# Taking the reciprocal of the softmax sums a little later, and scaling the weights behind the score copies

## The chip, the cores and the metric

The kernel runs on one core of one Trainium2 chip. The metric is the device time of one execution in microseconds (us). Five engines of the core work side by side, each through a queue of its own in a fixed order: TensorE (PE in the profile; PEld is its weight load), VectorE (DVE), ScalarE (ACT), GpSimd (POOL) and SyncE (SP, which here only issues DMAs). An instruction that waits holds up everything behind it in its queue.

## The reference

The reference has two stages, both in float32. The first is attention with a top-32 mask, for 8 batches of 8 heads, 576 positions and a head size of 64:

```python
scores = scale * np.matmul(q, k.transpose(0, 1, 3, 2))
kth = np.partition(scores, -top_k, axis=-1)[..., -top_k:-top_k + 1]
scores = np.where(scores >= kth, scores, -1000000000.0)
scores = scores - np.max(scores, axis=-1, keepdims=True)
attn = np.exp(scores)
attn = attn / (np.sum(attn, axis=-1, keepdims=True) + 1e-09)
return np.matmul(attn, v)
```

Its output, with the heads side by side, is x of 4608 x 512, and the second stage is a gated feed-forward block with a hidden width of 1536:

```python
g = x @ w_gate
silu = g * (1.0 / (1.0 + np.exp(-g)))
val = x @ w_val
return silu * val @ w_out
```

## The kernel before, in words

**Units.** The attention is cut into 160 units: 8 batches, 5 blocks of queries in each, 4 pairs of heads. The first four blocks of a batch have 128 queries, and such a unit treats two heads one after the other (two instructions of 128 x 576 wherever one head needs one). The fifth block has the last 64 queries; there the two heads of the pair share the 128 partitions, so that a unit has one "head". There are 128 units of two heads and 32 of one, and the 16 units in a row from one batch's start are followed by four single ones.

**Steps of a unit.** `scores` (L278) multiplies queries and keys on TensorE into four banks of PSUM (tile `s`, two for a single unit), and ScalarE copies them out to `sc` (L313, L299). `select` (L316) finds the 32 largest scores of each row on VectorE: four rounds of MAX8 (L328), which yields eight at a time, with MATCH_REPLACE8 (L332) between, which strikes those eight out and writes the rest to `e`. `penalize` (L338) has ScalarE scale the 32nd score (tile `top`, L344), form a penalty for everything below it (L348, into `e`), and GpSimd subtract the penalty from the scores (L351). `weigh` (L354) takes the exponential on ScalarE, in place in `e`, with the sum of each row as a side result in `tot` (L360), and adds the epsilon (L365). `normalize` (L368) takes the reciprocal of `tot` on VectorE (L372) and multiplies `e` by it on ScalarE (L375, one instruction for each head). `turn` (L377) transposes `e` on TensorE (tile `etps`, L387), copied out by ScalarE to `et` (L388). `values` (L398) multiplies by v, for two units together, into the bank `av` (L421), and ScalarE copies that to `xT` (L437), the input of the feed-forward block.

**Turns.** The main loop (L748) issues one turn after another. Turn n holds steps of several units: `select(n)`, `penalize(n - 1)`, `weigh(n - 1)`, and `turn(n - 2)`. In even turns it also holds `scores` of the units n + 1 and n + 2 and `values` of the units n - 4 and n - 3; odd turns have neither. The normalization of unit n - 1 is split over two turns: its reciprocal is the last VectorE instruction of turn n (`next(norm, None)`, L808), and its multiplications are run in turn n + 1 right behind `penalize` (`run(scaled)`, L772). Seen from turn n, ScalarE's queue so runs: top and penalties of unit n - 1, multiplications of unit n - 2, and then, in even turns, the four score copies of unit n + 1 and the copy of `av` to `xT`; then the exponentials of unit n - 1, the score copies of unit n + 2 in even turns, and the copies of the transposes of unit n - 2.

**Order and buffers.** All engines' queues keep the order in which the program issues (L817 to L830 chain the instructions of each engine but SP). `dve(k)` issues the next k steps of `select` for each head. `pieces` puts shares of the feed-forward block between (generator `feed`, L463; its matmuls are L477 for gate and value, L523 and L563 for the output), as many as a credit allows, which follows an estimate of each turn's other work. The attention's PSUM pool `ps_t` has five banks that are handed out in turn: two sets of four score banks in an even turn cannot both be there at once, so the second scores of that turn need banks that the copies of the first have freed. `e` has three buffers, `m` (the maxima) two.

**The first turns.** While the first units run, the feed-forward weights are loaded and rounded in pieces: a DMA into one of three buffers `w` (L106), three ScalarE instructions (L114, L116, L117), one on VectorE (L121), two on GpSimd (L122, L123). `early[0]()` (L779) issues the ScalarE part of such a piece inside the turn, ahead of the exponentials.

Of the kernel before, what the change touches and what calls it, by code (L numbers as in the profile page):

```python
# [25 lines left out]
def kernel(  # L26
# [174 lines left out]
    def rounding(n):  # L201
        for _ in range(n):
            next(weight, None)
# [70 lines left out]
    def n_heads(qt):  # L274

        return 1 if qt == J else 2

    def scores(n):  # L278
        b, qt, hp = units[n]
        slab = preps[b * NHP + hp]  # L280
        sc = work.tile([P, 2 * S], FP32, tag="sc", name="sc", bufs=3)
        halves = [slice(0, D), slice(D, P)]
        half = S // 2

        def bank():
            return ps_t.tile([P, 512], FP32, tag="t", name="s")


        if qt == J:
            banks = [bank() for _ in range(2)]  # L290
            for i, ps in enumerate(banks):
                for d in halves:
                    k0 = R + i * half
                    nc.tensor.matmul(  # L294
                        ps[d, 0:half], slab[d, S + R : S + 2 * R], slab[d, k0 : k0 + half]
                    )
            yield
            for i, ps in enumerate(banks):
                nc.scalar.copy(sc[:, i * half : (i + 1) * half], ps[:, 0:half])  # L299
        else:  # L300
            q0 = S + 2 * R + qt * P
            banks = []
            for i in range(2):
                for hh, d in enumerate(halves):
                    ps = bank()
                    banks.append((i + 2 * hh, ps))
                    k0 = (1 - hh) * R + i * half
                    nc.tensor.matmul(  # L308
                        ps[:, 0:half], slab[d, q0 : q0 + P], slab[d, k0 : k0 + half]
                    )  # L310
            yield
            for i, ps in banks:
                nc.scalar.copy(sc[:, i * half : (i + 1) * half], ps[:, 0:half])  # L313
        state[n] = dict(sc=sc)

    def select(n):  # L316

        nh = n_heads(units[n][1])
        sc = state[n]["sc"]
        m = small.tile([P, 2, TOP_K], FP32, tag="m", name="m", bufs=2)  # L320
        heads = [slice(t * S, (t + 1) * S) for t in range(nh)]
        e = work.tile([P, 2 * S], FP32, tag="e", name="e", bufs=3)
        state[n] |= dict(m=m, e=e, heads=heads)
        cur = sc
        rounds = TOP_K // 8
        for r in range(rounds):
            for t, hs in enumerate(heads):
                nc.vector.max(m[:, t, 8 * r : 8 * r + 8], cur[:, hs])  # L328
                yield
            if r < rounds - 1:  # L330
                for t, hs in enumerate(heads):
                    nc.vector.match_replace(  # L332
                        e[:, hs], m[:, t, 8 * r : 8 * r + 8], cur[:, hs], LOWEST
                    )
                    yield
                cur = e

    def penalize(n):  # L338

        st = state[n]  # L340
        sc, m, e, heads = st.pop("sc"), st.pop("m"), st["e"], st["heads"]
        nh = len(heads)
        top = small.tile([P, 2], FP32, tag="top", name="top")
        nc.scalar.mul(top[:, 0:nh], m[:, 0:nh, TOP_K - 1], BIG)  # L344
        bias = small.tile([P, 2], FP32, tag="bias", name="bias")
        nc.gpsimd.tensor_scalar_mul(bias[:, 0:nh], m[:, 0:nh, 0], -scale)
        for t, hs in enumerate(heads):
            nc.scalar.activation(  # L348
                e[:, hs], sc[:, hs], AF.Relu, bias=top[:, t : t + 1], scale=-BIG
            )  # L350
            nc.gpsimd.tensor_tensor(e[:, hs], sc[:, hs], e[:, hs], ALU.subtract)  # L351
        st["bias"] = bias

    def weigh(n):  # L354

        st = state[n]
        e, heads, bias = st["e"], st["heads"], st.pop("bias")
        tot = small.tile([P, 2], FP32, tag="tot", name="tot")
        for t, hs in enumerate(heads):
            nc.scalar.activation(  # L360
                e[:, hs], e[:, hs], AF.Exp, bias=bias[:, t : t + 1], scale=scale,
                accum_out=tot[:, t : t + 1],
            )
        nh = len(heads)
        nc.scalar.activation(tot[:, 0:nh], tot[:, 0:nh], AF.Identity, bias=eps[:])  # L365
        st["tot"] = tot

    def normalize(n):  # L368
        st = state[n]
        tot, e, heads = st.pop("tot"), st["e"], st.pop("heads")  # L370
        nh = len(heads)
        nc.vector.reciprocal(tot[:, 0:nh], tot[:, 0:nh])  # L372
        yield
        for t, hs in enumerate(heads):
            nc.scalar.mul(e[:, hs], e[:, hs], tot[:, t : t + 1])  # L375
# [83 lines left out]
    def flush(queue):  # L459
        while queue:  # L460
            queue.pop(0)()
# [201 lines left out]
    NU = len(units)  # L663
# [22 lines left out]
    def fetch(n):  # L686

        b, qt, hp = units[n]
        i = b * NHP + hp
        if qt == 0:  # L690
            yield from prep(i)
        if qt == J and i + NHP < len(pairs):
            load(i + NHP)

    def share(n):


        others = 0.0
        costs = [(m, 0.7) for m in scored(n) + valued(n)] + [(n - TURN, 0.6)]
        for m, cost in costs:  # L700
            if m >= 0:
                others += cost * (0.5 if units[m][1] == J else 1)
        if units[n + 3][1] == 0:
            others += 0.6

        beside = 6.4 if T[1] else 7.0
        return beside * n_heads(units[n][1]) / 2 - others

    def scored(n):

        ahead = [n + 1] if n < 2 else [] if n % 2 else [n + 1, n + 2]
        return [m for m in ahead if m < NU]

    def valued(n):

        behind = [] if n % 2 else [n - 4, n - 3]
        return [m for m in behind if 0 <= m < NU]

    def pieces(n):
        for _ in range(n):  # L720
            if credit[0] >= 1:
                credit[0] -= piece()

    def run(steps):
        for _ in steps:
            pass

    def finish_units(ns):
        values(ns)
        for n in ns:  # L730
            b, qt, hp = units[n]
            if qt == J and b + 1 < B:
                load_v((b + 1) * NHP + hp)
# [8 lines left out]
    load(2)  # L742
    credit = [0.0]
    no = iter(())
    scaled = no
    TURN = 2
    due = [2.0]
    for n in range(NU + 3):  # L748
        nh = n_heads(units[n][1]) if n < NU else 1
        topk = select(n) if n < NU else no  # L750
        norm = normalize(n - 1) if 0 <= n - 1 < NU else no
        nxt = [scores(m) for m in scored(n)]
        ahead = fetch(n + 3 if n else 2) if n + 3 < NU else no

        def dve(k, beside=True):

            for _ in range(k * nh):
                next(topk, None)
                due[0] += 5 / 6 if beside else 0
                if due[0] >= 1:  # L760
                    due[0] -= 1
                    rounding(1)

        if n >= NU - NHP:
            credit[0] = 8.0
        else:
            credit[0] = min(credit[0] + share(n), share(n) + 1)
        flush(on_act)
        if 0 <= n - 1 < NU:
            penalize(n - 1)  # L770
        flush(on_pool)
        run(scaled)  # L772
        if nxt:
            run(nxt.pop(0))
        if valued(n):
            finish_units(valued(n))
        if nxt:
            next(nxt[0])
        early[0]()  # L779
        if 0 <= n - 1 < NU:  # L780
            weigh(n - 1)
        if nxt:
            run(nxt.pop())


        dve(2, beside=False)
        if n == 0:
            run(ahead)
            load(3)
            ahead = fetch(3)  # L790
        if n < NHP:
            load_v(n)
        pieces(2)
        flush(on_act)
        dve(1)
        dve(1)
        if 0 <= n - TURN < NU:
            run(turn(n - TURN))

        flush(on_pool)  # L800
        next(ahead, None)
        pieces(1)
        next(ahead, None)
        dve(1)
        pieces(1)
        dve(2, beside=False)
        run(topk)
        next(norm, None)  # L808
        scaled = norm
        pieces(6)  # L810
    while piece():
        pass
# [48 lines left out]
```

## Time and profile before

| | |
|---|---|
| median of 9 runs | 1861.43 us |
| lowest and highest of them | 1856.46 and 1866.41 us |
| profiled execution: its own time | 1863.09 us |
| profiled execution: span | 1861.2 us |
| mean granted TensorE clock | 0.958 of full speed |
| busy: PE / PEld / DVE / ACT / POOL | 1713.5 / 1413.0 / 1451.6 / 1424.4 / 1043.9 us |

The span runs from the first to the last instruction. A busy time is the sum over an engine's instructions; a matmul's end is modelled, so that PE counts as busy also where a matmul is held up between its parts. The idle time before an instruction is put down to what released it. The chain of waits is followed back from the last instruction, at each step to what released it or to the instruction before it on its engine; what is on it took part in setting the end.

### The profile page before, as it was taken

The numbers are of one execution on the slowest core, as the hardware profiler recorded it, in microseconds if no ns is written. First come the engines' busy times: TensorE is split into PE (matmuls) and PEld (weight loads), VectorE is DVE, ScalarE is ACT, GpSimd is POOL, SyncE is SP. The second block draws the span as 40 slices with busy tenths as digits, with TensorE's granted clock in tenths as the row PEclk, the third lists the DMA queues.
The fourth block names the chain that finished last, engine by engine and source line by source line (L and its number), as shares of the span: only waits on it lengthen the run. The fifth ranks groups of instructions, "written<-read, shape, count | busy, mean of one in ns | idle before, by whom it ended". The sixth has DMA issues, their size and how long they took to land.

```text
span 1861.2 us, 30964 instructions
## 1 busy us (share of the span) xinstructions
PE 1713.5 (92%) x11012; PEld 1413.0 (76%) x11012; DVE 1451.6 (78%) x3084; ACT 1424.4 (77%) x3329; POOL 1043.9 (56%) x1058
## 2 busy tenths in 40 slices
PE   4448999799999999999999989999999999999999
PEld 2336677687888878887888868887788878788878
DVE  6986788997988788887888877877888878788300
ACT  6898788778788787788877786878787777787622
POOL 4777755545575636564556545555546554656444
PEclk6658999999999999999999999999999999999989
DMA  6433130001200030001200020000300010000000
GB/s 182 116 91 100 31 73 14 12 1 30 62 1 13 8 72 14 12 1 36 57 12 1 12 68 25 1 13 3 89 1 13 1 41 26 7 7 12 1 12 12
DMA packets 109307, 59.68 MB, mean 32 GB/s; under 512 B 88544, under 2 KB 96992, under 8 KB 109152
## 3 DMA queue, kind: packets, MB, share of 16 engines
q1 hardware_dynamic: 108016, 57.37, 11.9%
q8 instruction: 87, 1.43, 0.3%
q14 instruction: 68, 0.56, 0.1%
q10 hardware_dynamic: 1136, 0.33, 0.1%
HBM read 48.23 MB, written 9.44 MB: 31 GB/s over the span
## 4 chain that ended last, share of the span: by engine, by line
PE 72%; ACT 16%; POOL 6%; DMA 2%; DVE 1%; issue 1%; SPq 1%; ACTq 0%; POOLq 0%
PE f L477 37%; PE x_ps L563 8%; PE s L308 6%; PE av L421 6%; PE etps L387 6%; PE y_ps L563 5%; ACT e L348 4%; POOL e L351 3%; ACT e L375 2%; PE s L294 2%; ACT e L360 1%; ACT et L388 1%; ACT sc L313 1%; PE o_ps L523 1%; PE kqps L263 1%
## 5 line engine op out<-in xcount | busy, mean ns | idle before, releaser
L328 DVE MAX8 m<-e 128x8 f32<-128x576 f32 x864 | 616.0, 750 | 3.3
L351 POOL TENSOR_TENSOR e<-sc,e 128x576 f32<-128x576 f32 x288 | 403.0, 1419 | 346.1 <-ACT e L348 346.1
L332 DVE MATCH_REPLACE8 e<-m,e 128x576 f32<-128x576 f32 x576 | 424.3, 744 | 0.0
L477 PE MATMUL f<-xT,wg 128*128 128x256 f32 x1728 | 405.9, 384 | 0.0
L477 PE MATMUL f<-xT,wv 128*128 128x256 f32 x1728 | 405.6, 384 | 0.0
L477 PEld LDWEIGHTS f<-xT,wg 128*128 128x128 f32 x1728 | 326.7, 192 | 52.7 <-issue 8.5
L477 PEld LDWEIGHTS f<-xT,wv 128*128 128x128 f32 x1728 | 327.1, 192 | 51.5 <-issue 8.7
L505 POOL TENSOR_TENSOR h<-h,half_g 128x512 f32<-128x512 f32 x108 | 138.0, 1278 | 225.5 <-ACT h L504 225.5
L360 ACT ACTIVATE e<-e,bias 128x576 f32<-128x576 f32 x288 | 223.1, 780 | 49.4 <-POOL e L351 46.1
L308 PE MATMUL s<-kqT 64*128 64x288 f32 x1024 | 190.7, 467 | 68.7 <-ACT sc L313 49.2
L387 PE MATMUL etps<-ident,e 128*128 128x128 f32 (+1 forms) x1312 | 187.0, 285 | 50.7 <-ACT e L375 41.5
L387 PEld LDWEIGHTS etps<-ident,e 128*128 128x128 f32 (+1 forms) x1312 | 156.0, 145 | 88.1 <-ACT e L375 54.4
L348 ACT ACTIVATE e<-sc,top 128x576 f32<-128x576 f32 x288 | 209.7, 771 | 5.2
L332 DVE MATCH_REPLACE8 e<-m,sc 128x576 f32<-128x576 f32 x288 | 212.0, 743 | 0.0
L328 DVE MAX8 m<-sc 128x8 f32<-128x576 f32 x288 | 203.1, 742 | 9.3 <-ACT sc L313 9.3
L388 ACT COPY et<-etps 128x512 f32<-128x512 f32 (+1 forms) x448 | 182.5, 482 | 34.0 <-PE etps L387 33.7
L375 ACT ACTIVATE e<-e,tot 128x576 f32<-128x576 f32 x288 | 207.3, 762 | 0.0
L308 PEld LDWEIGHTS s<-kqT 64*128 64x128 f32 x1024 | 112.7, 199 | 116.6 <-ACT sc L313 58.3
L510 POOL TENSOR_TENSOR h<-h,val 128x512 f32<-128x512 f32 x108 | 137.8, 1276 | 108.8 <-ACT val L509 97.5
L372 DVE RECIPROCAL tot<-tot 128x2 f32<-128x2 f32 (+1 forms) x160 | 25.1, 157 | 198.8 <-ACT tot L365 198.8
L313 ACT COPY sc<-s 128x288 f32<-128x288 f32 x512 | 163.8, 400 | 5.3 <-PE s L308 5.3
L421 PE MATMUL av<-et,v 128*64 128x128 f32 (+1 forms) x2560 | 160.7, 270 | 0.0
(74 smaller groups left out, 2113.1 us busy)
## 6 DMA issues: line engine op xcount, KB each, us to landing
v<-in_v_dram SPq DMA_DIRECT2D x32, 256.0 KB, 3.2
kq_in<-in_k_dram SPq DMA_DIRECT2D x63, 128.0 KB, 3.1
kq_in<-in_q_dram SPq DMA_DIRECT2D x63, 128.0 KB, 3.2
w<-in_moe_w_gate_dram SPq DMA_DIRECT2D x12, 512.0 KB, 3.9
w<-in_moe_w_val_dram SPq DMA_DIRECT2D x12, 512.0 KB, 3.6
w<-in_moe_w_out_dram SPq DMA_DIRECT2D x12, 512.0 KB, 3.7
out_dram<-o SPq DMA_DIRECT2D x38, 128.0 KB, 2.4
out_dram<-o SPq DMA_DIRECT2D x16, 256.0 KB, 2.4
```

The lines of the kernel that those rows point to most:

```text
L308: nc.tensor.matmul(ps[:, 0:half], slab[d, q0 : q0 + P], slab[d, k0 : k0 + half])
L328: nc.vector.max(m[:, t, 8 * r : 8 * r + 8], cur[:, hs])
L332: nc.vector.match_replace(e[:, hs], m[:, t, 8 * r : 8 * r + 8], cur[:, hs], LOWEST)
L348: nc.scalar.activation(e[:, hs], sc[:, hs], AF.Relu, bias=top[:, t : t + 1], scale=-BIG)
L351: nc.gpsimd.tensor_tensor(e[:, hs], sc[:, hs], e[:, hs], ALU.subtract)
L360: nc.scalar.activation(e[:, hs], e[:, hs], AF.Exp, bias=bias[:, t : t + 1], scale=scale, accum_out=tot[:, t : t + 1],)
L375: nc.scalar.mul(e[:, hs], e[:, hs], tot[:, t : t + 1])
L387: nc.tensor.transpose(ps[0:kl, c * P : (c + 1) * P], e[:, k0 : k0 + kl], ident[:])
L388: nc.scalar.copy(et[0:kl, c0 : c0 + cn, :], ps[0:kl, 0 : cn * P].rearrange("p (c j) -> p c j", c=cn),)
L421: nc.tensor.matmul(av[d, i, 0:ql], weights_, moving, start=c == (0 if last else J), stop=c == (J if last else J - 1),)
L477: nc.tensor.matmul(ps[:, i, :], w[:, kc, m * P : (m + 1) * P], x[:, kc, :], start=(kc == 0), stop=(kc == KC - 1),)
L563: nc.tensor.matmul(ps, lhsT, T[i][m], start=m == 0, stop=m == MQ - 1)
```

## The change

The reciprocal of a unit leaves the end of a turn and comes into the next one, behind the first maxima of that turn's unit. The multiplications stay in the turn where they were, but move in ScalarE's queue: from right behind the penalties to right ahead of the exponentials, and so, in even turns, behind the four score copies and the copies of `av`, and in the first turns behind the three rounding instructions that `early[0]()` issues. `dve(2)` is split into two calls of `dve(1)` to make the place for the reciprocal.

```diff
-    scaled = no
     TURN = 2
     due = [2.0]
     for n in range(NU + 3):
         nh = n_heads(units[n][1]) if n < NU else 1
         topk = select(n) if n < NU else no
-        norm = normalize(n - 1) if 0 <= n - 1 < NU else no
+        norm = normalize(n - TURN) if 0 <= n - TURN < NU else no
...
         if 0 <= n - 1 < NU:
             penalize(n - 1)
         flush(on_pool)
-        run(scaled)
         if nxt:
             run(nxt.pop(0))
         if valued(n):
             finish_units(valued(n))
         if nxt:
             next(nxt[0])
         early[0]()
+        dve(1, beside=False)
+        run(norm)
         if 0 <= n - 1 < NU:
             weigh(n - 1)
         if nxt:
             run(nxt.pop())
-        dve(2, beside=False)
+        dve(1, beside=False)
...
         dve(2, beside=False)
         run(topk)
-        next(norm, None)
-        scaled = norm
         pieces(6)
```

## The prediction

> **What bounds the kernel now.** I read the chain of waits first, then the busy times, then who waits for whom, then single places of the chain and of the timeline.
>
> The page's busy times, the head of its chain of waits, and two of its groups:
>
> ```profile
> PE 1713.5 (92%) x11012; PEld 1413.0 (76%) x11012; DVE 1451.6 (78%) x3084; ACT 1424.4 (77%) x3329; POOL 1043.9 (56%) x1058
> ...
> PE 72%; ACT 16%; POOL 6%; DMA 2%; DVE 1%; issue 1%; SPq 1%; ACTq 0%; POOLq 0%
> ...
> L308 PE MATMUL s<-kqT 64*128 64x288 f32 x1024 | 190.7, 467 | 68.7 <-ACT sc L313 49.2
> ...
> L372 DVE RECIPROCAL tot<-tot 128x2 f32<-128x2 f32 (+1 forms) x160 | 25.1, 157 | 198.8 <-ACT tot L365 198.8
> ```
>
> PE sets the end. VectorE has the largest wait that the change touches, 198.8 us at the reciprocal, and 1% of the chain. So time is to be had where PE waits, and PE waits at the score matmuls (L308). Three stretches of the chain, in order of time (start, us, what), show how the moved multiplications (L375) lie in it. A middle turn:
>
> ```profile
> 1173.13 1.44 ACT e L348 x2
> 1174.57 1.33 ACT e L375 x2
> 1175.90 0.29 ACT sc L313
> 1176.19 0.04 issue
> 1176.24 1.64 PE s L308 x5
> ```
>
> PE's second scores need a bank that a score copy frees, and the copy stands behind both multiplications. The change takes them away from there. A turn at a batch's end:
>
> ```profile
> 649.62 2.36 PE av L421 x40
> 651.98 0.02 issue
> 652.00 0.37 ACT xT L437
> 652.37 1.53 ACT e L360 x4
> ```
>
> Here ScalarE waits for PE's `av`, and the exponentials follow at once: the multiplications were done while it waited. After the change they stand behind that wait, on the chain. And one of the first turns:
>
> ```profile
> 54.06 0.79 ACT e L348
> 54.84 0.07 issue
> 54.92 0.64 POOL e L351
> 55.56 0.72 issue
> 56.28 1.61 POOL e L351
> 57.89 1.52 POOL size L122
> ```
>
> The chain runs there from the penalty over GpSimd to the weight pieces, without a multiplication. Last, the timeline of PE at a turn whose wait is short:
>
> ```profile
> 1002.47 1.24 PE L308 MATMUL s<-kqT 64*128 64x288 f32 x8
> ...
> 1006.47 1.64 PE L308 MATMUL s<-kqT 64*128 64x288 f32 x8 [0.42 <-ACT sc L313]
> ```
>
> The second scores wait 0.42 us and then take 1.64 instead of 1.24 us, since each bank comes free one copy after the other: 0.40 us of hold-up that is counted as busy.
>
> **The change, part by part.** No instruction is added or removed, and PE's queue is untouched.
>
> *Score copies ahead of the multiplications (even turns).* The pair takes 1.43 us (0.76 in a single unit), so each copy, and each bank, comes that much earlier. From 285 us on, PE's timeline shows waits of the second scores for the copies of 0.23 us (5 times), 0.42 (6), 1.00 (1), 1.37 (7, one of them at L294) and 4.00 (1); one more of 1.09 at 351.65 I count as nothing, because the transposes behind it wait 1.13 for ScalarE anyway. Cut by up to 1.43 each: 1.15 + 2.52 + 1.00 + 9.59 + 1.43 = 15.7 us. The hold-up of 0.40 goes too in the eleven short ones: 4.4. In four of the turns with 1.37 ScalarE afterwards idles only 1.12 to 1.18 for the next feed-forward product, so the gain ends there: -0.8. Between 145 and 211 us the chain goes three times from L375 over a score copy to the scores (145.26, 177.93, 209.34); ScalarE's next wait for PE is 1.14, 0.41, and in the third the chain stays on PE: 1.14 + 0.41 + 1.43 = 3.0. Sum of the gain: 22.3 us.
>
> *Multiplications behind the wait for `av` (even turns).* Where ScalarE already waits for `av` at L437 the exponentials come a full pair later; where `av` ended shortly before, by what is missing. Added up over the even turns behind 200 us in ScalarE's and PE's timelines: 61 us of delay in 62 turns. That is the upper bound of what PE can lose, nothing the lower. Most of it is taken up by ScalarE's later idle time before the next odd turn's multiplications (1.0 to 2.9 us in most turns, waiting for L477's products and L387's transposes) and by the lead those multiplications have on the transposes (up to 2.3 us). It isn't taken up at the batch ends, where ScalarE doesn't idle: in the chain the step from `av` over L437 to L360 stands at single units at 452.7, 663.4, 874.7, 1086.2, 1304.0 and 1520.0 (6 x 0.76 = 4.6) and at 649.6 (1.43), and the two-headed turn before the single ones adds 1.2, 0.86, 0.87, 0.87 and 0.28 at the other five, and 0.6 at the first batch end: 4.7. Where the transposes come within 2.9 us of the exponentials (230, 533, 814, 1215 us) their second bank waits for the later score copies: 1.2. Sum of the loss: 11.9 us, nearer to the lower bound because most turns show the idle time that takes it up.
>
> *The transposes of an even turn* start 0.1 to 7.1 us behind the first exponential's old start, which is where the multiplications now end: no new wait. In odd turns nothing but rounding work lies between.
>
> *Reciprocal behind the first maxima.* The new order adds a wait: ScalarE's multiplication needs a reciprocal that stands behind two maxima (1.40 + 0.16 us) counted from VectorE's last maximum, while ScalarE spends 0.21 + 1.44 on top and penalties from the same moment. That is a margin of 0.1 us, and it matters only where ScalarE has to wait for VectorE at all: once, 3.5 us at 366.6. Behind the multiplication stand the exponentials, `tot` and the transposes' copies. Bounds: 0, and 8 x 0.6 us where a two-headed unit's maxima follow a single unit's penalty; I take 0. On VectorE itself the 73 waits shrink by at most the two maxima, 88 us in all, but the next MATCH_REPLACE8 then waits for a buffer `e` until PE's transposes are through (90.6 us already): cover for nothing, since VectorE is at the chain's 1%.
>
> *The first 145 us.* In even turns VectorE stalls about 3.5 us for a rounding piece (L121 for L114) that stood behind the multiplications; it now comes 1.43 us sooner, five times. Bounds: a gain of 7.2 and nothing. I take nothing: ScalarE works through such a turn without a gap (66.2 to 79.7 us) with the same instructions in another order, and the odd turn's length is penalty, GpSimd, DMA (3.6 us) and rounding; VectorE's stall is what is left over. Odd turns delay transposes by the rounding (1.7 us), which the exponentials' wait for GpSimd hides; if not, ScalarE's copies wait some tenths.
>
> *Queues of SP and GpSimd.* The DMAs are the same; a weight load and a k load of 0.4 to 0.6 us issue time change places early on, in either direction worth less than 0.6 us. GpSimd's queue is the same; its subtractions hang on L348, which doesn't move.
>
> **Sum.** 22.3 - 11.9 = 10.4 us. The profiled execution took 1863.09 us (span 1861.2, 1.9 around it), so 1852.7 on its own scale; it lies 1.7 above the median, which gives 1851.0.
>
> [...]
>
> **The rivals.**
> 1. *The wait for `av` takes the gain back (slower).* The place is L437 in even turns, with the multiplications now exposed behind it; the price is up to 61 us. It decides once more than 22.3 / 61 = 37% of that reaches PE; I counted 20%. At half, 30.5 - 22.3 = +8 us: 1869.6. For it: the batch ends, where ScalarE works without a gap for 20 us or more, and copies that free banks and `e` buffers later. Against: ScalarE idles 97.9 + 81.0 us at L502 and L509 for PE.
> 2. *A wash.* Every bank that comes earlier meets an equal delay: within 3.7 us of 1861.4. For it: both sums are of the same order.
> 3. *The first turns shorten too.* 7.2 us more, and a third of the loss is taken up (4): 1840. Against it: the chain, which has no VectorE there.
>
> **How the numbers follow.** A measurement of this kernel tells 0.2% (3.7 us) from no change. Chances: the forecast 0.43, rival 1 0.34, rival 2 0.13, rival 3 0.10. Faster is the forecast and rival 3, 0.53; same 0.13; slower 0.34. The range goes from rival 3 (1840) to rival 1 (1870); the forecast's own goes from 1844 to 1857, since its gain could be 15.7 + 3.0 and its loss 6 to 15.
>
> **What would show it.** Right: the idle time before L308 and L294 for the score copies falls by some 15 us behind 285 us, and second scores take 1.24 us; L437's wait for `av` grows from 27.7 towards 80 us; VectorE's wait at L372 drops to about 110 us while L332's for the transposes grows; turns keep their 12.4 and 13.4 us in the first 145 us. Wrong: PE's idle time before L387 and L263 at the batch ends grows by more than 20 us, or ScalarE waits at L375 for VectorE.

## The result and the profile after

The changed kernel took 1851.03 us (median of 12 runs, 1845.73 to 1854.74). The kernel before took 1861.73 us in this comparison (37 runs, 1856.46 to 1867.24). The ratio is 0.9936, with a 95% interval from 0.9927 to 0.9945. The forecast was 1851.0. Two further comparisons of the same two kernels, further down, gave 0.9957 and 0.9994, so the agreement to a tenth of a microsecond is better than it deserves.

The profiled execution after took 1850.61 us, its span is 1848.8 us (12.4 less than before), and the mean granted clock is 0.959 (before 0.958). From the page of the changed kernel: the busy times, the head of the chain, and two groups (busy time, mean ns of one, then the idle time ahead of them and what ended most of it).

```profile
PE 1699.8 (92%) x11012; PEld 1398.2 (76%) x11012; DVE 1453.9 (79%) x3084; ACT 1424.8 (77%) x3329; POOL 1044.1 (56%) x1058
...
PE 71%; ACT 16%; POOL 8%; issue 2%; DMA 2%; DVE 1%; SPq 0%; POOLq 0%; ACTq 0%
...
L387 PE MATMUL etps<-ident,e 128*128 128x128 f32 (+1 forms) x1312 | 190.2, 288 | 78.9 <-ACT e L375 63.5
...
L308 PE MATMUL s<-kqT 64*128 64x288 f32 x1024 | 179.5, 458 | 39.4 <-ACT sc L313 25.4
```

PE's idle time has not fallen: span minus busy is 147.7 us before and 149.0 after. It has moved. Ahead of the scores (L308) it went from 68.7 to 39.4 us, ahead of the transposes (L387) from 50.7 to 78.9. What came off is PE's busy time, 13.7 us, and 11.2 of that lies in L308, whose busy time was 190.7. Of these, 6.8 us are groups of matmuls that no longer stand half-issued while a bank is copied out (counted below); the rest of the 13.7 is in part less time at half clock (last section). So a saved wait of PE can show as busy time.

Who waits for whom, changed kernel, whole run (waiting instruction, releaser, total us, how often, longest):

```profile
DVE tot L372 <- ACT tot L365: 149.3, 65, 14.1
DVE e L332 <- PE etps L387: 95.4, 68, 2.5
...
ACT xT L437 <- PE av L421: 69.2, 55, 2.4
PE etps L387 <- ACT e L375: 63.5, 29, 7.8
...
PE s L308 <- ACT sc L313: 25.4, 7, 9.5
...
PE etps L387 <- ACT sc L313: 15.0, 14, 2.1
```

The same six were 198.8, 90.6, 27.7, 41.5, 49.2 and 8.5 us before. Cut at 300 us, the scores' wait for their copies fell from 17.8 to 0.6 us behind that point; the transposes' wait for the multiplications grew there only from 14.2 to 16.2, and their wait for the copies from 2.1 to 7.2. Most of the growth at the transposes is early: from 25.1 to 37.0 us ahead of 145 us, and from 2.1 to 10.4 between 145 and 300.

Three places show it. First the chain of the changed kernel in the middle turn that the prediction showed (start, us, what):

```profile
1170.80 1.17 PE s L308 x8
1171.97 2.33 PE av L421 x40
1174.30 0.04 issue
1174.34 1.65 PE s L308 x5
1175.99 3.65 PE f L477 x16
```

PE goes from `av` straight to the second scores. Penalties, multiplications and score copy are off the chain, and the wait of 1.37 us is gone. The scores still take 1.65 us here: the later banks are still being copied. Behind 285 us, 24 groups of second scores took 1.5 to 1.8 us before, 7 after; 17 times 0.40 is 6.8 us.

Second, the chain of the changed kernel at the batch end near 650 us:

```profile
647.35 2.36 PE av L421 x40
649.71 0.02 issue
649.73 0.37 ACT xT L437
650.10 1.34 ACT e L375 x2
651.44 1.52 ACT e L360 x4
```

The two multiplications, absent from this place before, now lie between `av` and the exponentials. In the whole chain this sequence (L437, then L375) occurs 20 times with 22.1 us of L375, against none before.

Third, PE's timeline of the changed kernel in two of the early turns:

```profile
164.11 2.18 PE L387 MATMUL etps<-ident,e 128*128 128x128 f32 x9 [4.51 <-ACT e L375]
166.09 5.05 PE L477 MATMUL f<-xT,wv 128*128 128x256 f32 x16
...
197.46 2.18 PE L387 MATMUL etps<-ident,e 128*128 128x128 f32 x9 [5.85 <-ACT e L375]
199.43 5.44 PE L477 MATMUL f<-xT,wg 128*128 128x256 f32 x16
```

Before, the transposes waited 1.07 and 1.06 us in these two turns, and the 16 products behind them took 3.62 us each time.

### The profile page after: what moved, and what is told of

Same layout as the page of the kernel before. It is cut to its first block, busy times and chain, and to the rows that moved or that the text cites. A ratio compares the mean times of both kernels' runs of the same rounds, so it can differ in the third digit from the quotient of the medians.

```text
span 1848.8 us, 31170 instructions
## 1 busy us (share of the span) xinstructions
PE 1699.8 (92%) x11012; PEld 1398.2 (76%) x11012; DVE 1453.9 (79%) x3084; ACT 1424.8 (77%) x3329; POOL 1044.1 (56%) x1058
## 4 chain that ended last, share of the span: by engine, by line
PE 71%; ACT 16%; POOL 8%; issue 2%; DMA 2%; DVE 1%; SPq 0%; POOLq 0%; ACTq 0%
PE f L477 36%; PE av L421 8%; PE x_ps L563 7%; PE s L308 6%; PE etps L387 5%; PE y_ps L563 5%; POOL e L351 3%; ACT e L360 2%; ACT e L348 2%; ACT e L375 2%; ACT sc L313 2%; PE s L294 1%; ACT et L388 1%; PE kqps L263 1%; ACT size L114 1%
## 5 line engine op out<-in xcount | busy, mean ns | idle before, releaser
L332 DVE MATCH_REPLACE8 e<-m,e 128x576 f32<-128x576 f32 x576 | 424.4, 744 | 0.0
L477 PE MATMUL f<-xT,wv 128*128 128x256 f32 x1728 | 401.1, 381 | 0.0
L387 PE MATMUL etps<-ident,e 128*128 128x128 f32 (+1 forms) x1312 | 190.2, 288 | 78.9 <-ACT e L375 63.5
L387 PEld LDWEIGHTS etps<-ident,e 128*128 128x128 f32 (+1 forms) x1312 | 158.0, 147 | 117.8 <-ACT e L375 84.8
L308 PE MATMUL s<-kqT 64*128 64x288 f32 x1024 | 179.5, 458 | 39.4 <-ACT sc L313 25.4
L332 DVE MATCH_REPLACE8 e<-m,sc 128x576 f32<-128x576 f32 x288 | 212.1, 744 | 0.0
L375 ACT ACTIVATE e<-e,tot 128x576 f32<-128x576 f32 x288 | 209.0, 771 | 0.0
L308 PEld LDWEIGHTS s<-kqT 64*128 64x128 f32 x1024 | 102.6, 197 | 86.6 <-ACT sc L313 31.1
L421 PEld LDWEIGHTS av<-et,v 128*64 128x64 f32 x2560 | 136.8, 140 | 7.6 <-ACT top L344 3.4
```

Source lines behind the costliest of these rows:

```text
L308: nc.tensor.matmul(ps[:, 0:half], slab[d, q0 : q0 + P], slab[d, k0 : k0 + half])
L332: nc.vector.match_replace(e[:, hs], m[:, t, 8 * r : 8 * r + 8], cur[:, hs], LOWEST)
L387: nc.tensor.transpose(ps[0:kl, c * P : (c + 1) * P], e[:, k0 : k0 + kl], ident[:])
L421: nc.tensor.matmul(av[d, i, 0:ql], weights_, moving, start=c == (0 if last else J), stop=c == (J if last else J - 1),)
L477: nc.tensor.matmul(ps[:, i, :], w[:, kc, m * P : (m + 1) * P], x[:, kc, :], start=(kc == 0), stop=(kc == KC - 1),)
```

## The experiments

No run leaves out or changes a part of the computation. All of them move the same three things: the reciprocal (L372), the multiplications (L375), and what stands ahead of these in ScalarE's queue. To compare places in time I use the start of ScalarE's `top` (L344), one in each turn. The "ends" are seven stretches of ten turns, from the `top` of unit 14 (near 219 us) on and every twenty turns, one around each of the first seven batches' ends; the "mids" are the six stretches of ten turns between them. The `top` of unit 14 is issued in turn 15, so each of these stretches lies one turn behind the ten turns that the mixtures of the third series choose. Summed lengths in us, each from one profiled execution:

| kernel | until unit 14 | ends | mids |
|---|---|---|---|
| before | 219.1 | 687.3 | 687.0 |
| changed | 221.6 | 689.9 | 670.9 |
| changed, third series | 220.5 | 693.0 | 672.4 |
| reciprocal alone | 219.6 | 685.9 | 681.9 |
| multiplications alone | 220.5 | 691.6 | 671.9 |
| between copies and `av` | 216.1 | 680.9 | 670.8 |
| between, second series | 217.1 | 681.0 | 672.5 |
| rounding behind | 215.5 | 695.6 | 672.3 |
| rounding behind, third series | 216.9 | 691.4 | 671.0 |
| late at the ends only | 216.6 | 693.0 | 670.9 |
| late between the ends only | 216.1 | 681.0 | 672.4 |

Two executions of one kernel differ by up to about 4 us in a column.

**Theories.** Mine: the copies ahead of the multiplications give some 22 us, the multiplications behind the wait for `av` take about 12 back at the batch ends, and the reciprocal is worth nothing. The rival: VectorE's shorter waits at the reciprocal bring the gain.

**The first series: each part by itself.** The kernel before took 1857.22 us on this chip.

*The reciprocal alone*, from the changed kernel; reciprocal behind the first maxima, multiplications back behind the penalties:

```diff
         flush(on_pool)
+        dve(1, beside=False)
+        run(norm)
         if nxt:
             run(nxt.pop(0))
...
         early[0]()
-        dve(1, beside=False)
-        run(norm)
```

> Only the reciprocal moves behind the next unit's first maxima; the multiplications stay right behind the penalties. Theory (the gain comes from the score copies): 1861 us, within 0.2% of the kernel before, PE's idle time before L308 for the score copies behind 285 us stays near 18 us, and VectorE's wait at L372 falls from 199 to about 150 us for nothing. Rival (the gain comes from VectorE, which waits less for the sums): about 1851 us, all of the change's gain.

Measured: 1855.18 us, ratio 0.9996 (0.9988 to 1.0005). Who waits for whom in it:

```profile
DVE e L332 <- PE etps L387: 148.9, 64, 3.4
...
DVE tot L372 <- ACT tot L365: 79.1, 54, 14.2
```

VectorE's wait at the reciprocal fell by 119.7 us (some 50 were expected), and the time stayed. 58 of these us are back at the next wait, MATCH_REPLACE8's for a buffer `e`, as the prediction named it. I did not follow the rest: VectorE has 1% of the chain here too.

*The multiplications alone*, from the kernel before:

```diff
         flush(on_pool)
-        run(scaled)
         if nxt:
             run(nxt.pop(0))
...
         early[0]()
+        run(scaled)
```

> Only the multiplications move behind the score copies and the copy of av; the reciprocal stays the last VectorE instruction of its turn. Theory (score copies): 1851 us, as the whole change, and PE's idle time before L308 for the score copies behind 300 us under 2 us. Rival (VectorE): 1861 us, as before the change.

Measured: 1852.91 us, ratio 0.9977 (0.9967 to 0.9987). Its wait at the reciprocal:

```profile
DVE tot L372 <- ACT tot L365: 254.8, 88, 14.1
```

This is 105.5 us more than in the changed kernel. The time came down by 4.3 us, between theory and rival, so this run alone decides nothing. In the next series the two kernels stand side by side.

*The multiplications between the copies and the copy of `av`*, from the changed kernel. This keeps the gain and takes away the exposure:

```diff
         if nxt:
             run(nxt.pop(0))
+        dve(1, beside=False)
+        run(norm)
         if valued(n):
             finish_units(valued(n))
         if nxt:
             next(nxt[0])
         early[0]()
-        dve(1, beside=False)
-        run(norm)
```

> As the changed kernel, but the multiplications stand right behind the first score copies, ahead of the copy of av (L437) and of the rounding instructions. Theory (the change gave back part of its gain at the wait for av and behind the rounding): the gain of some 20 us without the loss, 1839 to 1845 us, L437's wait for av back near 28 us of idle time, and PE's idle time before L387 in the first 300 us back near 35 us. Rival (those delays fall into time in which ScalarE waits for PE anyway): 1851 us, as the changed kernel.

Measured: 1834.87 us, ratio 0.9881 (0.9868 to 0.9895), 22.4 us less than before and below the range that was expected. ScalarE's timeline in it, in the same batch-end turn (start, us, line, operation, wait in brackets):

```profile
636.93 1.44 ACT L348 ACTIVATE e<-sc,top 128x576 f32<-128x576 f32 x2
638.58 0.88 ACT L299 COPY sc<-s 128x288 f32<-128x288 f32 x2 [0.21 <-PE s L294]
639.36 1.44 ACT L375 ACTIVATE e<-e,tot 128x576 f32<-128x576 f32 x2
641.40 0.37 ACT L437 COPY xT<-av 128x256 f32<-128x256 f32 x1 [0.60 <-PE av L421]
641.67 0.78 ACT L360 ACTIVATE e<-e,bias 128x576 f32<-128x576 f32 x1
```

and the same turn of the changed kernel:

```profile
645.26 1.44 ACT L348 ACTIVATE e<-sc,top 128x576 f32<-128x576 f32 x2
646.91 0.89 ACT L299 COPY sc<-s 128x288 f32<-128x288 f32 x2 [0.20 <-PE s L294]
649.73 0.37 ACT L437 COPY xT<-av 128x256 f32<-128x256 f32 x1 [1.93 <-PE av L421]
650.00 1.44 ACT L375 ACTIVATE e<-e,tot 128x576 f32<-128x576 f32 x2
651.34 0.77 ACT L360 ACTIVATE e<-e,bias 128x576 f32<-128x576 f32 x1
```

From the penalties to the exponentials it is 4.74 us in the first and 6.08 in the second. The multiplications fill ScalarE's wait for `av` in the first; in the second ScalarE idles 1.93 us and does them afterwards. Over the run L437's wait is 13.3 us in the first (28 were expected) and 69.2 in the second.

*The rounding behind the multiplications*, from the changed kernel, since the early turns had got slower:

```diff
-        early[0]()
         dve(1, beside=False)
         run(norm)
+        early[0]()
```

> As the changed kernel, but the rounding instructions of the first turns stand behind the multiplications again; the multiplications stay behind the copy of av. Theory (transposes that waited 4.5 and 5.9 us behind the rounding at 164 and 197 us made the first 20 turns 3.7 us longer than before): turn 20 starts some 5 us sooner than in the changed kernel and the run takes about 1846 us. Rival (the first turns' length is set by GpSimd and DMA, and later turns take up what is lost there): 1851 us.

Measured: 1848.69 us, ratio 0.9957 (0.9945 to 0.997). No run of the changed kernel stood beside it on that chip, so the time alone decides nothing. PE's timeline does for the first of the two turns:

```profile
161.03 1.43 PE L387 MATMUL etps<-ident,e 128*128 128x128 f32 x9 [1.27 <-ACT e L375]
162.30 3.62 PE L477 MATMUL f<-xT,wv 128*128 128x256 f32 x16
```

The wait of 4.51 is 1.27, and the products behind it take 3.62 us again. In the second turn the wait fell only from 5.85 to 3.52 us, and the products took 5.23.

**The second series: the changed kernel beside its parts.** The kernel before took 1861.22 us on this chip. The changed kernel and the multiplications alone were run unaltered.

> The changed kernel, unaltered, beside the next three on one chip, since the multiplications alone came out at a ratio of 0.9977 and the whole change at 0.9936, on two chips whose times for the kernel before differ by 4 us. Theory (the reciprocal's place is worth nothing): a ratio within 0.15% of that of the multiplications alone on this chip. Rival (the reciprocal's place is worth some 7 us once the multiplications are late, since the sums come later and VectorE waits for them): 0.3% or more below it.

Measured: 1852.67 us, ratio 0.9957 (0.9942 to 0.9971).

> Only the multiplications move; the reciprocal stays at the end of its turn. Theory: as the changed kernel on this chip, within 3 us. Rival: 6 to 8 us slower than it.

Measured: 1851.30 us, ratio 0.9952 (0.9933 to 0.9971). With and without the reciprocal's move it is the same time.

*Between, with the old reciprocal*, from the kernel before:

```diff
         flush(on_pool)
-        run(scaled)
         if nxt:
             run(nxt.pop(0))
+        run(scaled)
```

> The kernel before with one line moved: the multiplications right behind the first score copies, the reciprocal at the end of its turn as before. Theory (the reciprocal's place is worth nothing): a ratio of 0.988, as with the reciprocal behind the maxima. Rival (VectorE's wait for the sums counts): 0.3% or more above that.

Measured: 1837.07 us, ratio 0.9874 (0.9851 to 0.9896).

The kernel "between" with the new reciprocal was run again beside it.

> The multiplications right behind the first score copies, the reciprocal behind the maxima, beside the changed kernel on one chip. Theory: a ratio of 0.988 again, 10 to 14 us under the changed kernel. Rival (chips differ): less than 6 us under it.

Measured: 1838.25 us, ratio 0.9882 (0.9859 to 0.9904). The reciprocal's place is worth nothing in this order too. The rival theory falls in three pairs: alone, with the changed order, and with the order between.

**The third series: where the loss sits.** The kernel before took 1856.62 us on this chip. Two mixtures of "between" and the changed kernel, chosen by the turn:

```diff
+        late = n >= 14 and (n - 14) % 20 < 10
+        if not late:
+            dve(1, beside=False)
+            run(norm)
         if valued(n):
             finish_units(valued(n))
         if nxt:
             next(nxt[0])
         early[0]()
-        dve(1, beside=False)
-        run(norm)
+        if late:
+            dve(1, beside=False)
+            run(norm)
```

This one has the changed kernel's order at the ends only. The other has `>= 10` for `< 10`, which is that order between the ends only. In both, the turns ahead of turn 14 have the multiplications between.

> The multiplications right behind the first score copies, except in the ten turns around each batch's end (from turn 14 on, every 20 turns), where they stand behind the copy of av and the rounding as in the changed kernel. Theory (the wait for av costs only at the batch ends): the seven stretches of ten turns take 690 us in all, as in the changed kernel, against 681 with the multiplications between, and the run is 8 to 11 us slower than with them between everywhere, a ratio of about 0.993. Rival (the loss is spread over all even turns): half of that, 0.990 or less.

Measured: 1849.35 us, ratio 0.9961 (0.9948 to 0.9973), a larger loss than expected. The stretches took 693 us as against 681.

> The opposite: the multiplications behind the copy of av only in the turns between the batch ends, elsewhere right behind the first score copies. Theory: ScalarE's idle time takes the delay up there, so the run is within 2 us of the one with the multiplications between everywhere, a ratio of 0.988, though L437 waits for av nearly as long as in the changed kernel. Rival (spread): 5 us slower or more, 0.991.

Measured: 1834.81 us, ratio 0.9879 (0.9864 to 0.9893), as good as "between" everywhere, which did not stand beside it here but had 0.9881 and 0.9882 in the first two series.

ScalarE's wait for `av` in the one with the late order at the ends:

```profile
ACT xT L437 <- PE av L421: 40.1, 45, 2.4
```

and in the one with the late order between the ends:

```profile
ACT xT L437 <- PE av L421: 40.8, 36, 2.2
```

The same 40 us of waiting cost 14.5 us of time more in the one than in the other. A wait's length says nothing of its price; what stands on the chain does better. Its sequence L437, L375 occurs 15 times in the first (15.4 us) and 5 times in the second (6.7 us, which cost nothing that these runs can tell).

Last, the rounding behind the multiplications and the changed kernel itself, together on this chip.

> The changed kernel with the rounding behind the multiplications, beside the changed kernel on one chip. Theory (the transposes behind the rounding cost 5 us in the first turns, and that reaches the end): 4 to 6 us under the changed kernel. Rival (taken up later): within 2 us of it.

Measured: 1847.50 us, ratio 0.9953 (0.994 to 0.9967).

> The changed kernel, unaltered, for comparison on the same chip: a ratio of 0.993 to 0.996.

Measured: 1855.95 us, ratio 0.9994 (0.9986 to 1.0003). On this chip the change is a wash, outside what was expected. The kernel with the rounding behind the multiplications is 8.5 us faster here, more than expected; 3.6 of that are in the time until unit 14 in the traces, the rest is spread over stretches where the two orders do not differ. The changed kernel's trace here also lost 6.7 us more at half clock behind 300 us than its first trace (25.0 against 18.3, by the estimate of the last section), so the 8.5 us need not be the price of the rounding alone.

On this chip the account can be made: late order between the ends 1834.81 (21.8 below before); late at the ends instead +14.5; late in all the other turns as well +6.6; together the changed kernel's 1855.95. These steps are differences from run to run, so that their sum is right by construction; of the last, 3.9 us lie ahead of unit 14 by the table, where the rounding stands in the way.

**What came out as faster than both.** The multiplications behind the score copies but ahead of the copy of `av`: 0.9881, 0.9882 and, with the old reciprocal, 0.9874. It is the stablest of all: three chips, with the kernel late between the ends, agree within 0.001.

## Why the prediction was right or wrong

- *PE sets the end, VectorE doesn't: right, shown.* VectorE's wait at the reciprocal went from 79 to 255 us between these kernels, and the times did not follow it.
- *Reciprocal, 0: right, shown* by the three pairs. The changed kernel's waits hold none of ScalarE's multiplications for VectorE.
- *Score copies ahead, gain of 22.3 us: the size was right.* Where the loss is taken away the gain is 22.4, 23.0, 24.2 and 21.8 us (the three kernels "between" and the one late between the ends). By its terms: the wait of the second scores and L294 for the copies fell by 18.6 us behind 300 us (predicted 15.7); the hold-up by 6.8 (4.4).
- *The early turns: the step that failed is the rounding, which the prediction put at nothing.* The gain of 3.0 us between 145 and 211 us is there where nothing takes it back: with the multiplications between copies and `av`, unit 14's `top` comes 3.0 us earlier than before (216.1 for 219.1). In the changed kernel it comes 2.5 us later (1.4 and 2.1 in its other two traces). What lies between is the rounding ahead of the multiplications: put back behind them, with the multiplications still behind `av`, unit 14 comes 3.6 us earlier than before (2.2 in the second trace). The prediction said that in odd turns the rounding delays the transposes by 1.7 us, that the exponentials' wait for GpSimd hides it, and that otherwise some tenths are lost; it looked at the first 145 us only. Behind 145 us the odd turns still issue rounding, PE now has products to do, and the rounding itself waits for its DMA: in the first of the two turns L114 waited 1.35 us for its weights and started at 161.61 us, and the multiplications behind it at 163.30 (162.11 before). So the transposes waited 4.5 and 5.9 us, and the products behind them took 5.05 and 5.44 us for 3.62. This was a wait added ahead of an instruction in a queue, a kind of step that the prediction had to follow for the DMA too. Measured by these traces, it is a loss of some 4 to 6 us that the sum did not have.
- *Multiplications behind the wait for `av`, loss of 11.9 us at the batch ends: the place was right, the size somewhat low.* All seven single places that were named carry L375 behind L437 on the chain (0.67 six times and 1.34). The two-headed turns before five of them, counted with 0.28 to 1.2 us, carry the full 1.34. Priced by the runs: 14.5 us between late at the ends and late elsewhere; 9 to 12 us in the stretches at the ends (690 to 693 against 681).
- *Most of the 61 us is taken up elsewhere: right, shown* by the order late between the ends, which costs nothing that these runs can tell (its interval is 0.15% to either side).
- *The first 145 us: right.* The turns take 12.2 and 13.5 us (12.4 and 13.5 before), 0.7 us less by the last of them, though PE's wait for the multiplications grew there by 11.9 us.
- *The marks.* The mark of being wrong did not come: PE's idle time before L387 and L263 at the ends went from 10.8 to 19.1 us, less than the 20 us of growth that were named. Second scores were to take 1.24 us, and 7 still take some 1.65. L437's wait was to grow towards 80 us and is 69.2. L372's was to be about 110 and is 149.3. L332's was to grow with it and did by 4.8 only.
- *The sum.* 10.4 was predicted; 10.7, 8.6 and 0.7 us were measured in the three comparisons. Early and late errors (some 5.5 us, and 2.6) both went against the forecast, and the larger gain at the scores (18.6 + 6.8 for 15.7 + 4.4) went for it; that they partly cancel is luck. In the traced execution one more thing went for it: less time lost at half clock, which the sum did not contain (below). Rival 1's mechanism was real and lay close to its point of decision: on the third chip the loss against "between the ends" is 21.1 us, and 22.3 was the point; the 0.7 us that are left there are what rival 2 forecast.

What stays open: why the same change measured 0.9936, 0.9957 and 0.9994. The order between did not vary so: 0.9881, 0.9882, 0.9879. A difference in the time lost at half clock fits in direction, but by less than the whole. The median granted clock of the executions was 0.958 before and 0.960 after in the second comparison, and 0.960 before and 0.958 after in the third: by estimate up to some 4 us (0.002 of the span), once for the change and once against it. Over the executions of the kernel before in these two comparisons, though, the time moved by only 0.58 and 0.35 us for each us that the clock lost.

## What to carry to other kernels

In an in-order queue, put the copy that frees a bank for the bounding engine ahead of the queue's own work, and put that own work ahead of an instruction that will have to wait for a later product: the wait then hides it (at the batch end above, 1.44 us of multiplications went into a wait of 1.93 us, of which 0.60 was left). The first half of this rule was worth 22 us here, and leaving out the second half, and the rounding ahead of the multiplications, cost 14 to 21 of them. Price a new wait by whether it lies on the chain where the waiting engine has no idle time behind it, not by its length (40.1 and 40.8 us of waiting for `av` went with 1849.35 and 1834.81 us); and look also at what else the moved instruction now stands behind, down to the DMAs.

## What the runs showed of the hardware that was not expected

**TensorE's clock halves for a few microseconds in the middle of the run, after short waits.** PE's timeline of the kernel before at two like places:

```profile
1176.24 1.64 PE L308 MATMUL s<-kqT 64*128 64x288 f32 x8 [1.37 <-ACT sc L313]
1177.81 3.72 PE L477 MATMUL f<-xT,wv 128*128 128x256 f32 x16
...
1245.15 1.65 PE L308 MATMUL s<-kqT 64*128 64x288 f32 x8 [1.37 <-ACT sc L313]
1246.73 5.41 PE L477 MATMUL f<-xT,wv 128*128 128x256 f32 x16
```

The same wait, the same scores, and then 16 products in 3.72 us at the one and 5.41 at the other. Stretches of the kernel before around the second (us, busy time and count of PE, PEld, DVE, ACT, POOL, then the granted clock, DMA share and GB/s):

```profile
1245.00:1248.00 3.00, 2.85 (x12) 2.24 (x13) 0.00 (x0) 2.97 (x10) 3.00 (x3) 0.85 0.00 0
1248.00:1251.00 3.00, 3.00 (x10) 2.38 (x9) 1.48 (x3) 1.30 (x5) 0.13 (x1) 0.58 0.02 5
```

The granted clock drops, to 0.5 in the trace's clock record, for 3.41 us or a multiple of it: behind 300 us eight times in this trace, for 3.41 us (four times), 6.83 (three) and 10.24 (once), and once more at the end of the record. At 1246.73 us it cost 1.7 us (5.41 for 3.72). In the changed kernel it is at half from 162.16 to 168.98 us, from within the wait of 4.51 us on, and so for 2.9 of the 5.05 us that the products behind take:

```profile
160.00:164.00 4.00, 0.00 (x0) 0.00 (x0) 1.69 (x5) 2.65 (x6) 4.00 (x4) 0.77 0.19 76
164.00:167.40 3.40, 3.29 (x13) 3.02 (x14) 3.40 (x8) 3.37 (x9) 3.32 (x3) 0.50 0.00 0
```

Of the two waits of 1.37 us in the kernel before, then, one was followed by half the clock and the other was not.

The clock record also shows what tells the two places apart. In the traces of before and after, all its changes behind the first lie on one grid of 3.413 us. The wait at 1245 us (1243.78 to 1245.15) lies whole in one cell of that grid (1243.70 to 1247.11), and the next cell has half the clock; the wait at 1176 us (1174.87 to 1176.24) is cut in two by a border of cells at 1175.43. In these two traces, from 300 to 1800 us, a cell at full clock with less than 1.3 us without a matmul was followed by half clock in none of 829 cases, with 1.3 to 2.0 us in 9 of 19, and with 2.0 us or more in all 6. So here the drop went with how long PE idled within one cell, and the grid's place against the kernel's start differed: the record's first cell begins 11.48 us behind the span's start in the trace of before and 11.97 in that of after.

Half of each such stretch, added up from 300 us to the end of the clock record, is an estimate of the time lost to it: 23.1 us in the trace of before, 18.3 after, but 25.0 in the changed kernel's third trace, and 19.8 in "late between the ends". So two executions of the changed kernel differ by 6.7 us in this, with spans of 1848.8 and 1854.2. A single trace's span is not good to better than that, and of the 12.4 us between the two traces of the result 4.8 are of this kind; some of it may come from the waits that the change removed, some is chance, and these runs do not separate the two.

**Moved idle time counts.** PE's idle time ahead of the transposes rose by 28 us and ahead of the scores fell by 29, and the sum of both says nothing of the gain. That was in PE's busy time, 13.7 us less: 6.8 us are matmuls held up at a bank, and 4.8 us at most are time at half clock.
